# Linear attention into a routed expert layer on one core: the first batch's last products, W2's splits and two softmaxes put in other places

## The chip, the cores and the metric

The program runs on one core of a Trainium2 chip. The metric is the device time of one execution in microseconds, the median of several. The engines are named as the profile names them: PE (TensorE; PEld are its weight loads), DVE (VectorE), ACT (ScalarE), POOL (GpSimd) and SP (SyncE, which here only issues DMAs and loads registers). Each engine works through its own instructions in order, and an instruction starts when all that it waits for has been signalled.

## The reference, cut to what matters

The inputs are q, k and v of 8 batches, 8 heads, 576 positions and 64 columns, phi of 32 memory slots per head, an embedding for each of 8 experts, and the experts' weights w1 (512 by 1024) and w2 (1024 by 512).

```python
a = softmax(phi, axis=positions)
k_m, v_m = a.T @ k, a.T @ v                      # per head: 32 x 64
attn = softmax(q @ k_m.T / 8, axis=slots)        # per head: 576 x 32
x = (attn @ v_m), heads side by side             # 4608 tokens x 512
logits = (x / norm(x)) @ (emb / norm(emb)).T / tau
e, gate = argmax(logits), its softmax probability
out = gate * (relu(x @ w1[e]) @ w2[e])
```

## The kernel before, in words

A batch's 576 tokens are tiles of 128 (four, and one of 64 that overlaps: `T0`, `NT` = 5). The heads lie in two groups (`NG` = 2) of four, so the 8 x 32 slots are 2 x 128 partitions. The expert that most of a batch's tokens choose is worked out on the chip, its weights are loaded, and the whole batch goes through that one expert; tokens of other experts are counted and done at the end (`rest`), which this input does not need.

Two layers are fused with the attention's second product. `project` multiplies v_m with w1, `first` (16 steps: two halves of the tokens, eight blocks of 128 hidden columns, six matmuls each, L681) multiplies the attention weights with that and applies relu, and `second` (40 yields: the 64-token tile first, whose eight steps are the 0th to the 7th, then four tiles of eight steps) multiplies with w2. For precision each float32 operand is split into a rounded part and the rest: `wh`, `wl` of w2 (`split_w`, L651 and L652, one of eight row blocks at a time), `hh`, `hl` of the hidden layer (L684 by ACT and L687 by DVE, two per step), `gh`, `gl` of the projected w1 (L664, L665), `aT` of the attention weights (`part`, L641 by ACT or DVE and L642 by POOL).

The order of the work is written out by hand. `steps` fills two lists, and after each yield of `first` and `second` the list's entry is called, which appends instructions to the engines' queues. While batch b goes through its layers, these entries do for batch b+1 the scores' softmax (`fill`, `weigh`, `divide`, `turn`: per head group a chain on DVE, L64, L71, L73, L83 to L86, L92, with one exponential by ACT, L75), the attention's product with the values and the router's columns (`pairs`, L139, called in `visit`), the choice of the expert (`choose`, in `gather`, L208 to L212) and the load of its w1 and w2 (L442, L448), and for batch b+2 the softmax of phi (`largest` L457 on DVE, the exponential L472 on ACT, `shares` L483, and the transposes `flip`, L504, in `visit`).

What SP issues, in this order, in the first batch's second layer: `lay` writes the next batch's attention weights to DRAM (`td<-x`, L100, four DMAs per head group, behind `divide`), reads them back in token order (`ea<-td`, L104 and L106), `keep` saves two tensors (L633, L634), then the expert's number is loaded to a register (L212) and w1 (four DMAs of 512 KB, L442) and w2 follow. `project` of the next batch reads all four of w1's pieces.

The first batch has no batch before it, so it computes its own attention in pieces: tile 0 ahead of everything, tiles 1 and 2 (`attend(1, 2)`: products L119, transposes L172, `best`, then `norm`) between the halves of `project`, and tiles 3 and 4 by `attend(3, 4)` after step 2 of `first`. Its norms and gates (`late`: `root`, `gates`, six calls) follow steps 3 to 8; `idx` (L263) is on POOL. `split_w` of w2 follows step 2 (two blocks) and steps 9 to 14 (one each): POOL rounds blocks 0 to 5, ACT 6 and 7, POOL subtracts all eight.

Of the kernel before, what the change touches and what calls it, by code (L numbers as in the profile page):

```python
# [46 lines left out]
class Tokens:  # L47


    def __init__(self, k, b, pt):  # L50
        self.k, self.nc, self.b, self.pt = k, k.nc, b, pt
        wk = k.wk.tile
        self.lg = wk([P, NT, E], F32, tag="lg", name=f"lg{b}")
        self.ss = wk([P, NT], F32, tag="ss", name=f"ss{b}")
        self.s2 = wk([P, 2, NT], F32, tag="s2", name=f"s2{b}") if b else None
        self.m = wk([P, NT], F32, tag="m", name=f"m{b}")
        self.oh = wk([P, NT, E], BF16, tag="oh", name=f"oh{b}")
        self.po = {}
# [49 lines left out]
    def attend(self, *ti, pt=None, turned=True):  # L108

        k, nc, b = self.k, self.nc, self.b  # L110
        if b:
            self.open()
            self.pairs()
            return
# [12 lines left out]
    def open(self):  # L127

        self.ps = [self.pt([P, 512], f"po{self.b}_{n}") for n in range(4)]

    def pairs(self):
# [3 lines left out]
        for i in range(NT):  # L135
# [11 lines left out]
        self.room = ps[-1][:, 512 - E :]  # L147
        l2 = k.wk.tile([P, NT, E], F32, tag="l2", name=f"l2{b}")
        for n, i in enumerate((slice(0, 3), slice(3, NT))):
            for h, to in enumerate((self.lg, l2)):  # L150
                e = ps[2 * n + h][:, : 2 * d * (i.stop - i.start)].rearrange("p (i g m) -> p i m g", g=NG, m=d)
                e = e[:, :, D - D * h :][:, :, :E]
                nc.vector.tensor_reduce(out=to[:, i], in_=e, axis=AX.X, op=ALU.add)
        nc.vector.tensor_tensor(out=self.lg, in0=self.lg, in1=l2, op=ALU.add)
        self.best(*range(NT))
# [19 lines left out]
    def norm(self, *ti):  # L175
        k, nc = self.k, self.nc
        for i in ti:
            x = k.ea[:, i].rearrange("p (g k m) -> p g k m", g=NG, k=2)
            po = self.po[i] if self.b else [self.po[i].rearrange("p (g k m) -> p g k m", g=NG, k=2)[..., :D]]
            for h, y in enumerate(po):  # L180
                to = x[:, :, h] if self.b else x
# [8 lines left out]
                    accum_out=(self.s2[:, h] if self.b else self.ss)[:, i : i + 1],  # L190
# [42 lines left out]
    def root(self):  # L233
        k, nc, b, ss = self.k, self.nc, self.b, self.ss
        self.n = n = k.wk.tile([P, NT], F32, tag="n", name=f"n{b}")
        if b:
            nc.vector.tensor_tensor(out=ss, in0=self.s2[:, 0], in1=self.s2[:, 1], op=ALU.add)
# [38 lines left out]
class Kernel:  # L276
# [371 lines left out]
    def split_w(self, copy=None):  # L648
        j = self.halves
        x, h, l = self.w2s[:, j], self.wh[:, j], self.wl[:, j]  # L650
        (copy or self.nc.scalar.copy)(h, x)  # L651
        self.nc.gpsimd.tensor_tensor(out=l, in0=x, in1=h.bitcast(F32), op=ALU.subtract)  # L652
        self.halves += 1
# [89 lines left out]
    def steps(self, b, t, u):  # L743
# [4 lines left out]
        for j in range(8):  # L748
            at = first[j] if b else first[2] if j < 2 else first[7 + j]
            at.append(lambda j=j: self.split_w(self.nc.gpsimd.tensor_copy if b or j < 6 else None))  # L750
        if not b:
            late = t.late()
            first[2].append(lambda: t.attend(3, 4))
            first[3].append(lambda: t.norm(3, 4))
            first[4] += [t.total, lambda: self.load_kv(2)]

            for f in range(3, 9):
                first[f].append(lambda: next(late))
            first[12] += [lambda: self.keep(0), lambda: self.load_q(2)]
        if u:  # L760
# [19 lines left out]
            if m < B:  # L780
                for g in range(NG):
                    second[11 + 3 * g + o].append(lambda g=g: self.softmax(m, (g,)))
# [38 lines left out]
    def batch(self, b, t, u):  # L821
# [11 lines left out]
        for k, _ in enumerate(self.project(b, self.vT[b % 2]) if u else ()):  # L833
            if not b:
                for g in range(NG):
                    self.part(g, slice(HS, S) if k else slice(P, HS), self.nc.scalar.copy)
                if k:
                    t.norm(1, 2)
                else:
                    self.keys(1)  # L840
                    self.values(1)
                    t.attend(1, 2)
        if b and u:

            self.scores(b + 1)
# [255 lines left out]
```

## Time and profile before

| | us |
|---|---|
| median of 3 runs (lowest to highest) | 407.17 (406.46 to 407.32) |
| the profiled execution's own time | 406.74 |
| its span in the profile | 404.9 |
| PE busy / DVE / ACT / POOL | 393.5 / 262.3 / 157.2 / 171.2 |
| first batch's `first` begins, `second` begins | 32.38, 48.47 |
| second batch's `project` begins | 80.05 |

The span is what lies between the first and the last instruction that the profiler saw; the rest of the execution's own time lies around it. Matmuls are pipelined and their ends are modelled, so PE's busy share says little about waits of some tenths of a microsecond; the starts of its instructions in the timeline do. A timeline row gives the start, the duration, the engine, the line and the operation, and in brackets how long the engine had been idle and what ended that. PE's clock is granted at 0.998 of its upper level (2.4 GHz) over the span.

### The profile page before, as it was taken

To read this page: it belongs to the slowest core of one execution; us is meant where nothing else is said; L and a number is where in the kernel's file an instruction comes from. 1 tells how busy PE (TensorE), PEld (TensorE's weight loads), DVE (VectorE), ACT (ScalarE), POOL (GpSimd) and SP (SyncE) were. 2 spreads that over 40 slices of the span, in tenths; PEclk is the share of its full clock that TensorE was granted. 3 is DMA by queue.
4 is the path that set the end of the run, shared out by engine and by line. 5 is a ranking of instruction groups with operands and counts; after the bars stand their busy time and mean duration, and the time that the engine had idled before them with its cause. 6 is when DMAs were issued, how large, how long until landed. Compare 5 with 4: busy or idle time off the path is not lost. (4 is left out here: it accounts for less than half of the span.)

```text
span 404.9 us, 10350 instructions
## 1 busy us (share of the span) xinstructions
PE 393.5 (97%) x3933; PEld 318.5 (79%) x3933; DVE 262.3 (65%) x909; ACT 157.2 (39%) x430; POOL 171.2 (42%) x205
## 2 busy tenths in 40 slices
PE   7889999999999999999999999999999999999995
PEld 3458877798777978879787888879788897879784
DVE  4698795769664794758855795747936595745000
ACT  4366623165313633147311753137231561146110
POOL 1036563187133940369121961349303681329300
PEclk9999999999999999999999999999999999999999
DMA  8999927995679925995469926798359404790011
GB/s 265 345 363 357 375 61 183 342 358 212 149 255 386 349 46 132 346 384 234 74 215 389 387 82 160 251 388 338 56 137 361 178 2 81 249 396 6 14 53 56
DMA packets 69862, 91.24 MB, mean 225 GB/s; under 512 B 41800, under 2 KB 47688, under 8 KB 69808
## 3 DMA queue, kind: packets, MB, share of 16 engines
q1 hardware_dynamic: 66928, 82.00, 60.9%
q0 software_dynamic: 2688, 8.26, 5.8%
q8 instruction: 32, 0.52, 0.5%
q10 hardware_dynamic: 192, 0.28, 0.2%
q14 instruction: 22, 0.18, 0.1%
HBM read 71.19 MB, written 19.33 MB: 224 GB/s over the span
## 5 line engine op out<-in xcount | busy, mean ns | idle before, releaser
L681 PE MATMUL ph<-aT,gh 128*128 128x288 f32 x512 | 103.2, 297 | 0.0
L734 PE MATMUL py<-wh,hh 128*128 128x512 f32 x248 | 99.3, 400 | 0.0
L734 PE MATMUL py<-wh,hl 128*128 128x512 f32 x248 | 96.7, 390 | 0.0
L734 PE MATMUL py<-wl,hh 128*128 128x512 f32 x248 | 96.7, 390 | 0.0
L652 POOL TENSOR_TENSOR wl<-w2s,wh 128x512 fp32r<-128x512 f32 x64 | 85.1, 1330 | 5.0
L681 PEld LDWEIGHTS ph<-aT,gh 128*128 128x128 f32 x512 | 81.8, 188 | 1.7 <-DVE oh L162 0.8
L681 PE MATMUL ph<-aT,gl 128*128 128x288 f32 x256 | 75.4, 294 | 0.0
L687 DVE SCALAR_TENSOR_TENSOR hl<-ph,hh 128x288 fp32r<-128x288 f32 x128 | 55.8, 450 | 22.1 <-ACT hh L684 16.7
L739 ACT ACTIVATE ys<-py,gate 128x512 f32<-128x512 f32 (+1 forms) x39 | 25.1, 642 | 105.3 <-PE py L734 70.3
L684 ACT ACTIVATE hh<-ph 128x288 fp32r<-128x288 f32 x128 | 52.4, 417 | 31.9 <-PE ph L681 31.6
L868 POOL DMA_DIRECT2D out_dram<-ys x28 | 15.5, 553 | 106.1 <-ACT ys L739 69.4
L734 PEld LDWEIGHTS py<-wh,hh 128*128 128x128 f32 x248 | 46.5, 188 | 14.6 <-issue 4.9
L734 PEld LDWEIGHTS py<-wh,hl 128*128 128x128 f32 x248 | 46.6, 188 | 10.1
L734 PEld LDWEIGHTS py<-wl,hh 128*128 128x128 f32 x248 | 46.6, 188 | 9.0
L681 PEld LDWEIGHTS ph<-aT,gl 128*128 128x128 f32 x256 | 48.0, 188 | 0.0
L642 POOL TENSOR_TENSOR aT<-aw,aT 128x576 fp32r<-128x576 f32 (+3 forms) x20 | 23.7, 1204 | 48.4 <-DVE aT L641 42.8
L651 POOL CAST wh<-w2s 128x512 fp32r<-128x512 f32 x62 | 38.6, 622 | 1.0 <-DMA w2s<-w 0.9
L723 PE MATMUL py<-w2s,h 128*64 128x256 f32 x256 | 29.4, 382 | 0.0
L665 DVE TENSOR_TENSOR gl<-pg,gh 128x512 fp32r<-128x512 f32 x32 | 20.0, 684 | 8.7 <-ACT gh L664 8.7
L723 PEld LDWEIGHTS py<-w2s,h 128*64 128x64 f32 x256 | 17.7, 137 | 9.3 <-DVE hl L687 1.0
L472 ACT ACTIVATE ex<-ex,nm 128x576 f32<-128x576 f32 x16 | 12.3, 771 | 29.5 <-DVE nm L457 29.5
L664 ACT CAST gh<-pg 128x512 fp32r<-128x512 f32 x32 | 16.5, 599 | 10.5 <-PE pg L662 10.5
(180 smaller groups left out, 468.9 us busy)
## 6 DMA issues: line engine op xcount, KB each, us to landing
kx<-kv SPq DMA_DIRECT2D x32, 512.0 KB, 7.5
w2s<-w SPq DMA_DIRECT2D x32, 512.0 KB, 9.8
w1s<-w SPq DMA_DIRECT2D x28, 512.0 KB, 6.4
out_dram<-ys POOLq DMA_DIRECT2D x28, 256.0 KB, 6.1
qt<-qT SPq DMA_DIRECT2D x12, 576.0 KB, 8.8
ad<-aw SPq DMA_DIRECT2D x8, 576.0 KB, 12.5
td<-x SPq DMA_DIRECT2D x56, 72.0 KB, 2.1
ea<-td SPq DMA_DIRECT2D x7, 512.0 KB, 4.4
```

What stands on the lines that cost most here:

```text
L642: self.nc.gpsimd.tensor_tensor(out=al, in0=a, in1=ah.bitcast(F32), op=ALU.subtract)
L651: (copy or self.nc.scalar.copy)(h, x)
L652: self.nc.gpsimd.tensor_tensor(out=l, in0=x, in1=h.bitcast(F32), op=ALU.subtract)
L664: nc.scalar.copy(self.gh[:, g, f], ps[g])
L665: nc.vector.tensor_tensor(out=self.gl[:, g, f], in0=ps[g], in1=self.gh[:, g, f].bitcast(F32), op=ALU.subtract)
L681: nc.tensor.matmul(p, lhsT=w[:, g, fs], rhs=x[:, g, to], start=g == 0 and k == 0, stop=g == 1 and k == 2)
L684: nc.scalar.activation(self.hh[:, f, to], p, AF.Relu)
L687: nc.vector.scalar_tensor_tensor(out=self.hl[:, f, to], in0=p, scalar=0.0, in1=self.hh[:, f, to].bitcast(F32), op0=ALU.max, op1=ALU.subtract)
L723: nc.tensor.matmul(p[64 * j : 64 * j + 64], lhsT=self.h4[:, f], rhs=self.w2s[:, f, d * j : d * j + d], start=f == 0, stop=f == 7,)
L734: nc.tensor.matmul(p, lhsT=h[:, f, to], rhs=w[:, f], start=f == 0 and k == 0, stop=f == 7 and k == 2)
L739: nc.scalar.activation(y[:, :d], p, AF.Copy, scale=gate[:, i : i + 1])
L868: eng.dma_start(self.out[r : r + P], y)
```

## The change

For the first batch only: `attend(3, 4)` comes one step later and uses the 64 by 64 products of the later batches (`open`, `pairs`, `logits` for the last two tiles, then the transposes); its two square sums per tile go through `s2`. The transposes and norms of tiles 1 and 2 move behind step 0 of `first`, the second half of `project` behind step 1, so that two steps of `first` come ahead of it. `norm(3, 4)`, `total` and the six calls of `late` come one step later. All eight splits of w2 come behind the gates, one each behind steps 11 to 15 of `first` and 0 to 2 of `second`; POOL rounds blocks 0 to 2, ACT 3 to 7; POOL subtracts blocks 0 to 5, DVE 6 and 7. The maxima of phi for batch 2 are issued behind steps 0 and 1 of `second` and the exponentials behind steps 2 and 5 (before: all behind steps 18 and 21). For the later batches the only difference is that this softmax comes one step sooner (10 and 13 in place of 11 and 14).

```diff
     def attend(self, *ti, pt=None, turned=True):
-        if b:
-            self.open()
-            self.pairs()
+        if b or ti[0] == 3:
+            self.open(b)
+            if b:
+                self.pairs()
+            else:
+                self.pairs(1)
+                self.turned(*ti)
+                self.logits(1)
             return
...
-        for i in range(NT):
+        for i in range(3 * first, NT):
...
+    def logits(self, first=0):
...
-        nc.vector.tensor_tensor(out=self.lg, in0=self.lg, in1=l2, op=ALU.add)
-        self.best(*range(NT))
+        i = slice(3 * first, NT)
+        nc.vector.tensor_tensor(out=self.lg[:, i], in0=self.lg[:, i], in1=l2[:, i], op=ALU.add)
+        self.best(*range(3 * first, NT))
...
-        if b:
-            nc.vector.tensor_tensor(out=ss, in0=self.s2[:, 0], in1=self.s2[:, 1], op=ALU.add)
+        i = slice(0 if b else 3, NT)
+        nc.vector.tensor_tensor(out=ss[:, i], in0=self.s2[:, 0, i], in1=self.s2[:, 1, i], op=ALU.add)
...
-    def split_w(self, copy=None):
+    def split_w(self, copy=None, by=None):
...
-        self.nc.gpsimd.tensor_tensor(out=l, in0=x, in1=h.bitcast(F32), op=ALU.subtract)
+        (by or self.nc.gpsimd).tensor_tensor(out=l, in0=x, in1=h.bitcast(F32), op=ALU.subtract)
...
         for j in range(8):
-            at = first[j] if b else first[2] if j < 2 else first[7 + j]
-            at.append(lambda j=j: self.split_w(self.nc.gpsimd.tensor_copy if b or j < 6 else None))
+            at = first[j] if b else (first[11:] + second)[min(j, 7)]
+            copy = self.nc.gpsimd.tensor_copy if b or j < 3 else None
+            at.append(lambda j=j, copy=copy: self.split_w(copy, None if b or j < 6 else self.nc.vector))
         if not b:
             late = t.late()
-            first[2].append(lambda: t.attend(3, 4))
-            first[3].append(lambda: t.norm(3, 4))
-            first[4] += [t.total, lambda: self.load_kv(2)]
-
-            for f in range(3, 9):
+            first[3].append(lambda: t.attend(3, 4))
+            first[4] += [lambda: t.norm(3, 4), lambda: self.load_kv(2)]
+            first[5].append(t.total)
+
+            for f in range(4, 10):
                 first[f].append(lambda: next(late))
...
                 for g in range(NG):
-                    second[11 + 3 * g + o].append(lambda g=g: self.softmax(m, (g,)))
+                    if not b:
+                        second[g].append(lambda g=g: self.largest(m, g))
+                    second[10 + 3 * g if b else 2 + 3 * g].append(lambda g=g: self.softmax(m, (g,)))
...
-        for k, _ in enumerate(self.project(b, self.vT[b % 2]) if u else ()):
-            if not b:
-                for g in range(NG):
-                    self.part(g, slice(HS, S) if k else slice(P, HS), self.nc.scalar.copy)
-                if k:
-                    t.norm(1, 2)
-                else:
-                    self.keys(1)
-                    self.values(1)
-                    t.attend(1, 2)
-        if b and u:
-
-            self.scores(b + 1)
+        project = self.project(b, self.vT[b % 2]) if u else ()
+        if b:
+            list(project)
+            if u:
+                self.scores(b + 1)
+        else:
+            self.part(0, slice(P, HS), self.nc.scalar.copy)
+            next(project)
+            self.part(1, slice(P, HS), self.nc.scalar.copy)
+            self.keys(1)
+            self.values(1)
+            t.attend(1, 2, turned=False)
+            first[0] += [lambda: t.turned(1, 2), lambda: t.norm(1, 2)]
+            first[1].insert(0, lambda: list(project))
+            for g in range(NG):
+                first[1].append(lambda g=g: self.part(g, slice(HS, S), self.nc.scalar.copy))
```

## Rows read from the trace of the kernel before

**Rows 1.** The page: busy time, share of the span, instructions by engine.
```profile
PE 393.5 (97%) x3933; PEld 318.5 (79%) x3933; DVE 262.3 (65%) x909; ACT 157.2 (39%) x430; POOL 171.2 (42%) x205
```
**Rows 2.** Timeline of PE, first batch's opening: start us, us, engine, line, operation, count.
```profile
30.77 0.66 PE L172 MATMUL tt<-ident,aw 128*128 128x128 f32 x4 [0.36 <-ACT kT L551]
...
34.86 1.09 PE L119 MATMUL po<-vv,aw 128*128 128x136 f32 x8
35.78 0.60 PE L172 MATMUL tt<-ident,aw 128*128 128x128 f32 x4
36.14 0.51 PE L681 MATMUL ph<-aT,gh 128*128 128x288 f32 x2
```
**Rows 3.** Timeline of PE where the first batch's second layer meets the visit.
```profile
63.55 0.39 PE L734 MATMUL py<-wh,hl 128*128 128x512 f32 x1
64.40 0.28 PE L504 MATMUL po<-ident,ex 64*128 64x64 f32 x2 [0.46 <-ACT ex L472]
...
65.10 1.48 PE L139 MATMUL po<-vv,aw 64*64 64x72 f32 x80
```
**Rows 4.** Waits of PE over the span: us in total, times, longest us.
```profile
PE po L504 <- ACT ex L472: 0.6, 2, 0.5
```
**Rows 5.** Timeline of PE and its weight loads: `project` of the second and third batch.
```profile
80.05 2.28 PE L662 MATMUL pg<-w1s,vT 64*32 64x512 f32 x32
80.42 0.23 PEld L662 LDWEIGHTS pg<-w1s,vT 64*32 64x32 f32 x10 [0.20 <-DMA w1s<-w]
...
128.03 1.95 PE L662 MATMUL pg<-w1s,vT 64*32 64x512 f32 x32
```
**Rows 6.** L442's DMAs issued from 70 to 73 us: issue to landing.
```profile
DMA to landing us min/median/max: 6.0/7.1/8.4
```
**Rows 7.** Timeline of SP, first batch's second layer.
```profile
58.13 5.12 SPq L100 DMA_DIRECT2D td<-x  x8
65.10 0.39 SPq L104 DMA_DIRECT2D ea<-td  x1
...
70.30 2.70 SPq L442 DMA_DIRECT2D w1s<-w  x4
```
**Rows 8.** Waits of the DMA queue SP from 57 to 71 us.
```profile
SPq L100 <- DVE x L86: 14.8, 2, 13.9
```
**Rows 9.** Timeline of DVE, first batch's second layer.
```profile
49.97 0.77 DVE L64 STREAM_TRANSPOSE x<-sT 128x576 f32<-128x576 f32 x1
...
51.56 1.56 DVE L73 TENSOR_TENSOR x<-x,mx 128x576 f32<-128x576 f32 x1
...
54.63 1.51 DVE L73 TENSOR_TENSOR x<-x,mx 128x576 f32<-128x576 f32 x1
...
60.28 0.76 DVE L86 TENSOR_TENSOR x<-x,z 128x576 f32<-128x576 f32 x1
61.15 0.78 DVE L92 STREAM_TRANSPOSE aw<-x 128x576 f32<-128x576 f32 x1
...
61.98 1.37 DVE L457 TENSOR_REDUCE nm<-ex 128x1 f32<-128x576 f32 x2
```
**Rows 10.** Timeline of POOL around the first batch's splits.
```profile
44.76 0.61 POOL L651 CAST wh<-w2s 128x512 fp32r<-128x512 f32 x1
...
51.23 4.29 POOL L652 TENSOR_TENSOR wl<-w2s,wh 128x512 fp32r<-128x512 f32 x3
```
**Rows 11.** Timeline of ACT at the end of the first batch's first layer.
```profile
48.40 0.72 ACT L651 CAST wh<-w2s 128x512 fp32r<-128x512 f32 x1
48.91 0.53 ACT L684 ACTIVATE hh<-ph 128x288 fp32r<-128x288 f32 x1
```
**Rows 12.** Durations in ns, min/median/max, of two of SP's instructions, whole span.
```profile
L106 SPq DMA_DIRECT2D ea<-td x14: 509/597/1318, 65.5 to 343.8; - x14
L212 SPq TENSOR_LOAD <-seli x8: 264/280/913, 20.7 to 346.7; - x8
```
**Rows 13.** The page: a product of half a tile with its square sum.
```profile
L182 DVE CUSTOM_DVE_ANT_1 ea<-po,ea 128x128 f32<-128x128 f32 x70 | 15.3, 285 | 0.0
```

More of the change, by code (lines that the diff above doesn't have):

```diff
@@ L54, in __init__ @@
         self.ss = wk([P, NT], F32, tag="ss", name=f"ss{b}")
-        self.s2 = wk([P, 2, NT], F32, tag="s2", name=f"s2{b}") if b else None
+        self.s2 = wk([P, 2, NT], F32, tag="s2", name=f"s2{b}")
         self.m = wk([P, NT], F32, tag="m", name=f"m{b}")
@@ L125, in attend, with open, pairs @@
         self.best(*ti)
-    def open(self):
-        self.ps = [self.pt([P, 512], f"po{self.b}_{n}") for n in range(4)]
-    def pairs(self):
+    def open(self, all=True):
+        self.ps = [self.pt([P, 512], f"po{self.b}_{n}") if all or n > 1 else None for n in range(4)]
+    def pairs(self, first=0):
         k, nc, b, d, ps = self.k, self.nc, self.b, D + E, self.ps
         at = lambda i, h: ps[2 * (i // 3) + h][:, 2 * d * (i % 3) :][:, : 2 * d].rearrange("p (g m) -> p g m", g=NG)
-        for i in range(NT):
+        for i in range(3 * first, NT):
             for g in range(NG):
@@ L147, in pairs @@
         self.room = ps[-1][:, 512 - E :]
+        if not first:
+            self.logits()
+    def logits(self, first=0):
+        k, nc, b, d, ps = self.k, self.nc, self.b, D + E, self.ps
         l2 = k.wk.tile([P, NT, E], F32, tag="l2", name=f"l2{b}")
-        for n, i in enumerate((slice(0, 3), slice(3, NT))):
+        for n in range(first, 2):
+            i = slice(3, NT) if n else slice(0, 3)
             for h, to in enumerate((self.lg, l2)):
@@ L178, in norm @@
             x = k.ea[:, i].rearrange("p (g k m) -> p g k m", g=NG, k=2)
-            po = self.po[i] if self.b else [self.po[i].rearrange("p (g k m) -> p g k m", g=NG, k=2)[..., :D]]
+            two = isinstance(self.po[i], list)
+            po = self.po[i] if two else [self.po[i].rearrange("p (g k m) -> p g k m", g=NG, k=2)[..., :D]]
             for h, y in enumerate(po):
-                to = x[:, :, h] if self.b else x
+                to = x[:, :, h] if two else x
                 nc.vector.tensor_tensor_reduce(
@@ L189, in norm @@
                     op1=ALU.add,
-                    accum_out=(self.s2[:, h] if self.b else self.ss)[:, i : i + 1],
+                    accum_out=(self.s2[:, h] if two else self.ss)[:, i : i + 1],
                 )
```

## The prediction

> **What bounds the kernel now.** The page says that PE is busy for 97% of the span [rows 1], which looks like a kernel that only less matrix work can shorten. Because ends of matmuls are modelled, I read PE's timeline by starts instead, looking for places where PE stood still. In the third to last batches there are none that this change could touch: in the whole span PE waited only twice for the softmax of phi [rows 4]. So the time to be won lies in the first batch and at its border to the second, and there are three such places.
>
> First, at 30.77 the transposes of tiles 1 and 2 start after 0.36 us of idle PE [rows 2]. Second, at 64.40 the visit starts after 0.46 us in which PE waited for the exponential of phi [rows 3]. Third, and this decides: `project` of the second batch takes 2.28 us where the same 32 matmuls take 1.95 in the third, and the weight loads in it resume at 80.42, released by the DMA of w1 [rows 5]. PE is there at 80.05 and waits 0.33 us in the middle for the last of w1's four pieces. That piece was issued near 72 and needed 8.4 us, the longest of the four [rows 6, 7].
>
> So behind the first batch PE is not the only bound. A second chain arrives at the same place a little later than PE. Followed backwards: w1 is issued from 70.30 on SP; before it stand the two kept tensors and `ea<-td` from 65.10; before that the eight `td<-x`, issued from 58.13 to 63.25 [rows 7]; and these wait for DVE's L86, the last step of `divide` [rows 8], whose second instance ends at 60.28 + 0.76 = 61.04 [rows 9]. DVE in turn works from 49.97 on: `fill`, maximum, subtraction for one head group, the same for the other, then the two divides [rows 9]. Whatever DVE is given ahead of 49.97 makes w1 later; whatever PE saves before 80.05 only makes it wait longer there.
>
> **The change, part by part.** The sum is made against the profiled execution, 406.74 us (span 404.9 and 1.84 around it). The median of the runs, 407.17, is 0.43 above it.
>
> *PE's opening.* Step 0 of `first` takes the place of the idle 0.36 us, since by then PE no longer needs the copy that the transposes waited for. The products of tiles 3 and 4 now take 0.92 us (34.86 to 35.78) [rows 2]. In 64 by 64 tiles there are 2 tiles x 2 groups x 4 matmuls x 2 passes = 32 instructions; the visit's 80 take 1.48 us [rows 3], so 32 take 0.59, and 0.33 is saved at most. The array is switched to the small tiles and back, which no row prices alone; between 0 and the whole 0.33 I take half, 0.17. The two gaps together make 0.53; I take 0.45 for PE's arrival at the second layer, because the later logits and norms leave DVE a little closer to the steps (bounds 0.2 and 0.7).
>
> The Trainium skill's page "TensorEngine Tiling (Array Packing)", in "Theoretical Speedup", allows up to a factor of two for each dimension of 64, which on columns alone (72 in place of 136) would save 0.43 us here; "Key Properties" of the same page has each change of tiling mode drain the engine, which speaks against it. Rows 3 stand nearer to the second. By the first, PE's gain would be 0.7 and the end the same, as it lies ahead of the wait for w1.
>
> *Logits and norms.* Four products of half a tile at 0.285 us [rows 13] replace two whole ones, and two short additions are new. They lie on DVE beside the steps of `first`; what covers them is that PE needs a step's result only four steps later. If that cover went, under 1 us of PE's gain would go with it, again ahead of the wait for w1.
>
> *POOL.* Its splits started at 44.76 behind the gates and ended at 55.52 [rows 10]. Now it does six subtractions and three roundings from about the same moment: 3 x (0.61 + 1.3) + 3 x 1.43 = 10.0, so it ends near 55 again. The third last block is then only just in time for PE. If PE waits there, by up to a microsecond, it waits less for w1.
>
> *ACT.* One of its two roundings (0.51 from start to start, 48.40 to 48.91 [rows 11]) no longer stands before the last relu. With PE's 0.45 that puts DVE's last `hl` about 0.65 sooner, and DVE is free at 49.97 - 0.65 = 49.3. Three roundings for blocks 4 to 6 then follow on ACT, and block 6 is ready near 50.45.
>
> *DVE, ahead of `fill`.* One maximum of phi: 1.37 / 2 = 0.69 [rows 9], to 50.0. Then DVE's subtraction of block 6, queued behind it, waits for ACT until 50.45, and everything behind it waits too. The trace has no such subtraction on DVE with both inputs in SBUF. The nearest rows are two of that kind on 576 columns: L86 takes 0.76 with POOL idle, L73 takes 1.56 and 1.51 while POOL subtracts back to back [rows 9, 10]. For 512 columns that is 0.68 or 1.36. POOL is subtracting at that moment, so I take 1.36; 0.68 stays the lower end. Second maximum 0.69, subtraction of block 7 again 0.68 to 1.36. `fill` starts at 50.45 + 2 x 1.36 + 0.69 = 53.9 (lower end 52.5) where it was 49.97: +3.9 (+2.5).
>
> *DVE, behind it.* The two L73 no longer run against POOL, which is done near 55: they should take 0.8 each in place of some 1.45, which gives back 1.3 (0.65 if the first still meets POOL, as it does in the lower case). The divides end 2.6 later, or 1.9. I take 2.4. The two maxima that stood at 61.98 are gone from there, but nothing on this chain stood behind them.
>
> The Trainium skill's page "SBUF — State Buffer", "Who interferes with whom", says that VectorE and GpSimd share one pair of ports as an exclusive lock, so that the second to issue blocks until the first is done. Rows 9 and 10 agree with a slowdown of that size. By that rule a subtraction on DVE could cost up to 0.68 + 1.43 = 2.1 us, and the sum would be 1.5 us higher.
>
> *The visit.* Its wait for the exponential (0.46) goes, as both are done by 54. What is late next is `turn` of the second group: it ended at 61.93 [rows 9] and will end near 64.3, while PE wants it at 65.10 - 0.46 - 0.45 = 64.2. So about 0.1 to 0.3 of the 0.46 comes back as a new wait.
>
> *SP.* No DMA changes its place in the queue. All of it from `td<-x` on moves with L86: +2.4. In this chain stand two instructions that take unusually long in the first batch only: a small `ea<-td` at 1.318 (0.6 otherwise) and the load of the expert's number at 0.913 (0.28 otherwise) [rows 12]. Nothing shows why; if they go with the new moment, 1.35 us is taken back. I take 0.4 for that: w1 is issued and lands 2.0 us later, the last piece at 82.4.
>
> *Later batches.* The softmax one step sooner: nothing, PE has no wait there [rows 4].
>
> *Sum.* PE reaches `project` at about 79.4 instead of 80.05 and waits until 82.4 instead of 80.42. From there all is as before, 2.0 later: 406.74 + 2.0 = 408.7 for the profiled kind of run, 407.17 + 2.0 = 409.2 for the median.
>
> **The rivals.** *Faster.* w1 lands before PE wants it. Then PE keeps 0.45, the 0.46 of the visit and the 0.33 of `project`: 1.24, a median of 405.9. The place is SP's first w1 DMA: PE wins only if it is issued before 70.3, and by over 0.2% (0.8 us, about what a measurement of this kernel can tell from no change) only if by 69.5. For it: SP's two slow instructions. Against it: DVE gets 1.4 us of maxima and at least 1.4 us of subtractions ahead of `fill`, and only 1.3 + 0.65 come back. Chance 0.12.
>
> *No change.* The lower case of DVE (+1.9, or +1.2 if both L73 are freed as well) meets SP's whole slack of 1.35: w1 comes between -0.15 and +0.6, and the median is 407.0 to 407.8. Chance 0.14.
>
> *Slower still.* Each subtraction on DVE waits out one of POOL's: +1.5 on the sum less what SP takes back, about 410.3. I count this within slower, with 0.1 of its chance. The forecast's own case has 0.64.
>
> That the change does not do what it says is not to be expected of the order, as each queue runs in the order written; only the sooner softmax of the later batches is without effect.
>
> **How the numbers follow.** The likeliest case is 409.2, from 408.0 (lower DVE case, half of SP's slack) to 410.2. The range of 8 in 10 reaches down into "no change" to 407.0 and up to 410.3; what it leaves out is the faster rival and the top of the slowest. Slower by over 0.2%: 0.74; within: 0.14; faster: 0.12.
>
> **What would show it.** In the changed profile the row at 30.77 has lost its wait, and L504 its wait for the exponential. L64 starts between 52.5 and 54 with two L457 and two subtractions of `wl` on DVE ahead of it, the latter near 1.4 us. The second L86 ends near 63.4, w1's first DMA is issued near 72.3, and the weight loads of the second `project` wait about 3 us for the DMA of w1. I am wrong if w1 is issued at 70.3 or sooner, if `project` takes its 1.95 us, or if L64 starts before 51.

## The result and the profile after

The changed kernel takes 410.06 us (median of 10 runs, 409.03 to 411.86) where the kernel before, run beside it, takes 407.25 (10 runs, 405.75 to 408.29). The ratio is 1.0082, with a 95% interval of 1.0062 to 1.0102: about 3.3 us slower. The forecast was 409.2, that is +2.0, with a range up to 410.3; 407.25 x 1.0082 is 410.6. The profiled execution of the changed kernel took 411.66 (span 409.8), 1.6 above its median, while that of the kernel before lay 0.5 below its own. So the traces differ by 4.9 us, of which 1.6 to 2.1 belong to these two executions. In both traces PE's clock stands at its upper level up to the last 1.6 us (mean 0.998 in both), so the clock has no part in what they differ by.

PE's busy share on the page is 97% as before [rows 1], with 24 more matmuls and as many more weight loads:

```profile
PE 398.3 (97%) x3957; PEld 318.9 (78%) x3957; DVE 263.1 (64%) x917; ACT 158.6 (39%) x433; POOL 167.4 (41%) x200
```

What grew is seen where `project` waits. First its line in the kernel before, over the whole span: us waited, times.

```profile
  DMA w1s<-w: 0.5, 2
```

The same line (now L676) in the changed kernel:

```profile
  DMA w1s<-w: 5.8, 6
```

The timeline of PE's weight loads in the second batch's `project` of the changed kernel (answers to [rows 5]):

```profile
80.06 0.14 PEld L676 LDWEIGHTS pg<-w1s,vT 64*32 64x32 f32 x4 [0.17 <-PE tk L561]
81.00 0.14 PEld L676 LDWEIGHTS pg<-w1s,vT 64*32 64x32 f32 x4 [0.80 <-DMA w1s<-w]
83.05 0.14 PEld L676 LDWEIGHTS pg<-w1s,vT 64*32 64x32 f32 x4 [1.92 <-DMA w1s<-w]
84.15 0.19 PEld L676 LDWEIGHTS pg<-w1s,vT 64*32 64x32 f32 x16 [0.95 <-DMA w1s<-w]
```

The four loads of w1 that `project` reads, from issue to landing (answers to [rows 6]):

```profile
DMA to landing us min/median/max: 6.5/7.7/8.8
```

PE arrives at 80.06 as before (80.05), and now waits for the second, third and fourth piece of w1; it goes on behind the last at 84.15, where it was 80.42. That is +3.73, and it is there that the second batch falls behind. The chain that leads to it, in the timelines of DVE and SP (answers to [rows 7, 9]):

```profile
50.04 0.74 DVE L471 TENSOR_REDUCE nm<-ex 128x1 f32<-128x576 f32 x1
51.19 0.93 DVE L666 TENSOR_TENSOR wl<-w2s,wh 128x512 fp32r<-128x512 f32 x1 [0.40 <-ACT wh L665]
52.05 0.74 DVE L471 TENSOR_REDUCE nm<-ex 128x1 f32<-128x576 f32 x1
52.71 1.11 DVE L666 TENSOR_TENSOR wl<-w2s,wh 128x512 fp32r<-128x512 f32 x1
53.74 0.77 DVE L64 STREAM_TRANSPOSE x<-sT 128x576 f32<-128x576 f32 x1
...
55.33 1.52 DVE L73 TENSOR_TENSOR x<-x,mx 128x576 f32<-128x576 f32 x1
...
58.36 0.76 DVE L73 TENSOR_TENSOR x<-x,mx 128x576 f32<-128x576 f32 x1
...
63.27 0.76 DVE L86 TENSOR_TENSOR x<-x,z 128x576 f32<-128x576 f32 x1
...
61.12 5.42 SPq L100 DMA_DIRECT2D td<-x  x8
69.23 0.39 SPq L104 DMA_DIRECT2D ea<-td  x1
...
73.18 2.46 SPq L456 DMA_DIRECT2D w1s<-w  x4
```

The links are: end of the divides 61.04 to 64.03 (+2.99); from there to `ea<-td`, which waits for the last `td` to land, 4.06 to 5.20 (+1.14); from `ea<-td` to w1's first piece 5.20 to 3.95 (-1.25); from w1's first piece to PE going on 10.12 to 10.97 (+0.85). Sum +3.73.

Elsewhere in the first two layers, on PE (answers to [rows 2, 3]):

```profile
30.85 0.51 PE L695 MATMUL ph<-aT,gh 128*128 128x288 f32 x2
...
36.15 0.73 PE L144 MATMUL po<-vv,aw 64*64 64x72 f32 x32
36.81 0.66 PE L185 MATMUL tt<-ident,aw 128*128 128x128 f32 x4
...
64.13 0.39 PE L748 MATMUL py<-wh,hl 128*128 128x512 f32 x1
64.45 0.28 PE L518 MATMUL po<-ident,ex 64*128 64x64 f32 x2
```

The wait for the exponential is gone from the visit, and the 32 small products take 0.66 from start to start. The opening does not show in absolute times, because in this execution the whole opening runs late, from before anything that the change touches: DVE's first L92 starts at 19.23 where it was 18.29, and its turn of the next 448 columns (L92) at 28.79 where it was 27.85. Counted from the latter, the first full tile of the second layer starts 23.58 later; it was 24.22. The new opening thus saves PE 0.64.

Behind the second batch two more places are slower. In the third batch the first layer starts 3.83 later than before, and `project` of the fourth 4.18: the 16 last matmuls of `acc` took longer by 0.34 (first row the kernel before, second the changed kernel; both timelines of PE).

```profile
161.00 0.45 PE L522 MATMUL acc<-kl,eT 64*32 64x128 f32 x16
```
```profile
164.83 0.79 PE L536 MATMUL acc<-kl,eT 64*32 64x128 f32 x16
```

And the last batch's `project` takes 2.70 where it took 1.95, waiting for w1:

```profile
357.87 1.95 PE L662 MATMUL pg<-w1s,vT 64*32 64x512 f32 x32
```
```profile
362.02 2.70 PE L676 MATMUL pg<-w1s,vT 64*32 64x512 f32 x32
...
362.81 0.57 PEld L676 LDWEIGHTS pg<-w1s,vT 64*32 64x32 f32 x18 [0.62 <-DMA w1s<-w]
```

The traces' 4.9 us are so 3.73 + 0.35 + 0.75, and 0.1 of small things.

### The profile page after: what moved, and what is told of

Its sections match the earlier page's. It is cut to its first block, busy times and chain, and to the rows that moved or that the text cites. A ratio compares the mean times of both kernels' runs of the same rounds, so it can differ in the third digit from the quotient of the medians.

```text
span 409.8 us, 10406 instructions
## 1 busy us (share of the span) xinstructions
PE 398.3 (97%) x3957; PEld 318.9 (78%) x3957; DVE 263.1 (64%) x917; ACT 158.6 (39%) x433; POOL 167.4 (41%) x200
## 5 line engine op out<-in xcount | busy, mean ns | idle before, releaser
L666 POOL TENSOR_TENSOR wl<-w2s,wh 128x512 fp32r<-128x512 f32 x62 | 81.6, 1318 | 4.8
```

Source lines behind the costliest of these rows:

```text
L666: (by or self.nc.gpsimd).tensor_tensor(out=l, in0=x, in1=h.bitcast(F32), op=ALU.subtract)
```

## The experiments

Two theories were held against each other. The first is the forecast's: DVE's work ahead of `fill` makes SP's chain late, and with it w1. The second: PE itself waits somewhere else (in its new opening, for W2's blocks, in transfers). A third came up on the way. Each ratio below is to the kernel before, run on the same chip beside it (406.9 to 407.4); 0.1% is 0.4 us.

**The opening alone.** In the changed kernel W2's splits and the softmax of phi go back to their old places:

```diff
-            at = first[j] if b else (first[11:] + second)[min(j, 7)]
-            copy = self.nc.gpsimd.tensor_copy if b or j < 3 else None
+            at = first[j] if b else first[2] if j < 2 else first[7 + j]
...
-                    if not b:
-                        second[g].append(lambda g=g: self.largest(m, g))
-                    second[10 + 3 * g if b else 2 + 3 * g].append(...)
+                    second[10 + 3 * g if b else 18 + 3 * g].append(...)
```

> Of the change only the products of tiles 3 and 4 in 64 by 64 tiles and the two sooner steps of the first layer; W2's splits and the two softmaxes of phi stand where they stood before. Theory (what is put ahead of DVE's fill makes w1 late, and PE waits for it): fill starts at 49.4 to 50.0, the last piece of w1 lands at 80.0 to 80.5, and whatever PE gains in the opening is waited away there: 406.8 to 407.5. Rival (the new opening itself costs: in the changed kernel's trace step 0 of the first layer took 0.207 us per matmul and DVE's opening was 0.9 us late): 408 or more, with PE behind the kernel before at the second layer.

Measured: 1.0039 (1.0014 to 1.0064), +1.6 us, and `fill` starts at 51.94, not at 49.4 to 50.0. That is the rival's number, but not by its mechanism. PE stood still once in the first layer, and the three timelines (PE, DVE, POOL) say why:

```profile
42.66 0.53 PE L695 MATMUL ph<-aT,gh 128*128 128x288 f32 x2 [1.53 <-DVE hl L701]
...
41.13 1.11 DVE L39 TENSOR_SCALAR nrg<-nrg 128x5 int32<-128x5 int32 x1
42.16 0.44 DVE L701 SCALAR_TENSOR_TENSOR hl<-ph,hh 128x288 fp32r<-128x288 f32 x1
...
40.95 1.27 POOL L666 TENSOR_TENSOR wl<-w2s,wh 128x512 fp32r<-128x512 f32 x1
```

A step on 5 columns that takes 0.17 elsewhere took 1.11 and ended at 42.24, with POOL's subtraction (42.22). The norms now come one step later and meet POOL's early splits. So the opening and the splits' new places belong together: the later splits are what lets the opening gain.

**The splits alone**, in the kernel before: the changed lines of `split_w` and its places, nothing else.

> Of the change only the places and engines of W2's splits (POOL rounds three blocks, ACT five, POOL subtracts six, DVE two). Theory: two subtractions of 0.9 to 1.1 us on DVE and a wait for ACT put fill at 51.8 to 52.6, the divides and w1 follow by 1.3 to 2.0 us, 408.5 to 409.4. Rival (POOL's six blocks come too late and PE waits in the second layer): PE is late before 64 us by 0.3 us or more, w1 is no later than that, 407.5 to 408.2.

Measured: 1.0054 (1.0032 to 1.0076), +2.2 us, as the theory had it in number, but not by its sum. `fill` starts at 53.36, about 1 later than expected, since the two subtractions, back to back, take 2.91. PE waits about 1 us for w1, and it waits more at the visit:

```profile
66.23 0.37 PE L504 MATMUL po<-ident,ex 64*128 64x64 f32 x2 [2.57 <-ACT ex L472]
...
67.39 2.41 PE L139 MATMUL po<-vv,aw 64*64 64x72 f32 x80
```

The maxima of phi stood behind the divides, and were now late. That is what moving them ahead of `fill` cures. The 80 products behind the wait took 2.41 where they took 1.48 [rows 3], because PE's clock was granted at its lower level (1.2 GHz, 0.50 of full speed) from 66.0 to 69.4, after PE had stood still for 2.57. This row gives the stretch from 66 to 69.4, the busy time of PE, PEld, DVE, ACT and POOL, then the granted clock (0.50), the DMAs' share and GB/s:

```profile
66.00:69.40 3.40, 3.17 (x86) 3.05 (x90) 0.99 (x7) 2.04 (x7) 0.54 (x1) 0.50 0.36 39
```

From the transposes `te` to the first product behind the visit that costs 1.33 (3.34 in place of 2.01). Of the twelve executions, the three with a mean clock of 0.999 or 1.000 took 407.7 to 408.0 us, the nine with 0.992 to 0.996 took 408.9 to 410.8. So a good part of the 2.2 is the clock, which the theory did not have, and the agreement in number is in part luck.

**The maxima alone**, in the kernel before:

```diff
-                    second[11 + 3 * g + o].append(lambda g=g: self.softmax(m, (g,)))
+                    if not b:
+                        second[g].append(lambda g=g: self.largest(m, g))
+                    second[11 + 3 * g + o if b else 2 + 3 * g].append(...)
```

> Of the change only the two maxima of phi behind steps 0 and 1 of the second layer, with the exponentials behind steps 2 and 5. Theory: two maxima of 0.69 us put fill at 51.2 to 51.5, w1 lands 0.9 to 1.5 us later, the visit's wait of 0.46 us goes but PE waits that much longer for w1: 408.0 to 408.8. Rival (the chain behind fill has slack that takes it in): 406.8 to 407.4.

Measured: 0.9977 (0.9957 to 0.9996), 0.9 us faster: both ranges were missed. The trace is of the longest of its 12 executions (408.20, 1.8 above their median). In it `fill` starts at 52.17, later than expected, but the second L73 no longer met POOL (0.76 in place of 1.51), and w1's first piece was issued at 70.50, only 0.20 later than before [rows 7]:

```profile
66.73 0.39 SPq L104 DMA_DIRECT2D ea<-td  x1
67.17 1.16 SPq L106 DMA_DIRECT2D ea<-td  x2
...
70.50 2.89 SPq L442 DMA_DIRECT2D w1s<-w  x4
```

SP's two slow instructions [rows 12] were not there: from `ea<-td` to w1 3.77 in place of 5.20. Up to w1's first issue the chain thus had the slack that the prediction's rival "no change" counted on, and the visit's wait is gone. But in this execution PE still waited for w1, whose second issue took 1.20 and whose last piece landed at 81.98 (80.37 before):

```profile
82.02 0.18 PEld L662 LDWEIGHTS pg<-w1s,vT 64*32 64x32 f32 x16 [1.48 <-DMA w1s<-w]
```

So the trace shows the slack, not the gain; where the 0.9 of the median comes from is not shown.

**w1 first on SP**, in the changed kernel: the reads of td behind w1, the kept tensors behind w2.

```diff
-        if g < NG - 1:
-            return
+        if g == NG - 1 and b != 1:
+            self.back()
+
+    def back(self):
...
         self.again()
+        if u.b == 1:
+            u.back()
         self.load_w2(e)
...
-            second[22 + o] += [self.parts, lambda: self.keep(c)]
+            second[22 + o].append(self.parts)
+            second[22 + o if b else 26].append(lambda: self.keep(c))
```

> The whole change, and on SP the first batch's three small reads of the tokens' values and the two kept tensors come behind the four loads of w1 instead of ahead of them; the reads then stand ahead of w2, the kept tensors behind it. Nothing else moves, so DVE's fill is still at 53 to 54. Theory (all of the loss is w1 behind SP's queue): w1's first piece is issued near 69 as soon as the expert's number is known, the last lands before 80.2, PE does not wait for it, and the visit's 0.46 us and the 0.33 us before w1 are gained: 405.8 to 406.7. Rival (the loss is in PE's second layer or in slower transfers): 408.5 or more.

Measured: 1.0172 (1.0142 to 1.0202), +7.0 us. w1 was issued at 68.54 and had landed before PE came, as expected; but the reads of td, queued behind it, now landed late, and DVE's norms with them:

```profile
79.06 0.29 DVE L200 CUSTOM_DVE_ANT_1 ea<-po,ea 128x128 f32<-128x128 f32 x1 [7.83 <-DMA ea<-td]
```

ACT waited 11.0 for the logits behind these norms, and PE stood still for 3.06 in the middle of `project` until ACT went on. Then PE's clock was at its lower level from 86.4 to 89.8, and from the 25th product of `project` to the first layer it took 3.56 (1.99 before). The order `ea` ahead of w1 is therefore needed; what may move is the kept tensors.

**The kept tensors behind the weights**, in the changed kernel (the last three lines of the diff above).

> The whole change, and on SP the two kept tensors (ad, vd) of the first batch come behind the loads of w1 and w2; the three reads of td stay ahead of w1, since behind it (the run before) the reads landed only at 79 and DVE's norms waited 7.8 us for them. Theory (w1 is late because of what SP has ahead of it): the two kept tensors take 1.31 us of SP in the changed kernel, so w1's first piece is issued about 1.3 us sooner against the divides, the last lands 1.0 to 1.5 sooner, and the time is 408.6 to 409.2. Rival (the landing of w1 is set by the transfers themselves, or DVE's norms set the end): 409.7 to 410.5, no different from the changed kernel.

Measured: 1.0025 (1.0003 to 1.0046), 408.27. It gives back 2.3 of the 3.3 us by the ratios, more than was expected. From `ea<-td` to w1 it is now 2.50 (3.95 in the changed kernel), and the wait of L676 for w1 over the span falls from 5.8 to 4.3. SP's timeline:

```profile
68.91 0.39 SPq L104 DMA_DIRECT2D ea<-td  x1
69.35 1.19 SPq L106 DMA_DIRECT2D ea<-td  x2
71.41 2.10 SPq L456 DMA_DIRECT2D w1s<-w  x4
```

This bears out one half of the first theory: nothing but SP's order was touched, and the time followed w1. It does not show that DVE's new work is what made w1 late, as the kept tensors stood ahead of w1 before the change too.

**The same with the maxima alone**, in the kernel before.

> The kernel before with two edits alone: the two maxima of phi behind steps 0 and 1 of the second layer (exponentials behind 2 and 5), and the two kept tensors behind the loads of w1 and w2 on SP. Theory: PE keeps the 0.46 us of the visit, and w1, 1.3 us sooner on SP, makes PE wait 0.3 us or less in the second project: 405.0 to 405.8, against 406.4 with the maxima alone. Rival (SP's order is not what holds w1): 406.2 to 406.8.

Measured: 0.9976 (0.9954 to 0.9998), no different from the maxima alone. Here L662 waits for w1 neither in the second batch nor in the last: w1 is there first, so that a still earlier one buys nothing. These two versions are the ones that beat both kernels.

**No subtraction on DVE**, in the changed kernel:

```diff
-            at.append(lambda j=j, copy=copy: self.split_w(copy, None if b or j < 6 else self.nc.vector))
+            at.append(lambda j=j, copy=copy: self.split_w(copy))
```

> The whole change, but POOL subtracts all eight blocks (DVE none). Theory: without two subtractions and the wait for ACT, 2.5 us, DVE's fill starts 2.3 to 2.6 us sooner, both L73 meet POOL again and cost 1.5 more, so the divides and w1 come 0.9 to 1.3 sooner; POOL ends near 59 and PE waits 1 to 2 us for blocks 6 and 7 before the visit, which takes that much out of the wait for w1: 408.6 to 409.5. Rival (POOL's late blocks set the end through PE): 410 or more, with no wait for w1 left in project.

Measured: 1.0042 (1.0023 to 1.0061), 409.19, as expected: 1.6 of the 3.3 us come back by the ratios without DVE's two subtractions, which bears out the other half. `fill` starts at 50.15, both L73 meet POOL (1.72 and 1.51), and PE waits for POOL's last blocks (waits between 51 and 64.6):

```profile
PEld py L748 <- POOL wl L666: 1.8, 2, 1.2
...
PE py L748 <- POOL wl L666: 0.8, 1, 0.8
```

**The maxima put back**, in the changed kernel: opening and splits together.

> The whole change, but the maxima and exponentials of phi stand where they stood before (behind steps 18 and 21 of the second layer): the new opening and W2's splits together. Theory: DVE has its two subtractions but not the maxima ahead of fill, which starts 0.3 to 0.7 us sooner than in the changed kernel (the subtractions wait for ACT anyway); the visit waits 2.5 to 3.5 us for the exponentials, as with the splits alone: 409.3 to 410.3. Rival (the maxima, not the subtractions, delay the divides): 408 or less.

Measured: 1.0109 (1.0080 to 1.0138), +4.4 us, 2 more than the middle of what was expected. The visit's wait is the 2.82 that was foreseen; the splits' two subtractions, back to back, take 1.36 in the mean (0.96 and 1.76), the upper price of the prediction.

```profile
69.18 0.28 PE L518 MATMUL po<-ident,ex 64*128 64x64 f32 x2 [2.82 <-ACT ex L486]
```

Here too PE's clock was at its lower level for a while: from 30.0 to 33.4, after PE had stood still for 2.38 until the first batch's w1 came. From the first `tk` product to the fourth of `first` it took 3.41, where the opening alone took 1.83. That 1.6 is most of the 2 in this execution; the mean clock of all six lies between 0.991 and 0.995 (0.996 to 0.999 in the changed kernel), and where the others lost it is not recorded.

**The second tile's output held back**, in the changed kernel, because it lies among the `td` writes:

```diff
+            elif not b and i == 1:
+                self.held = lambda: eng.dma_start(self.out[r : r + P], y)
...
+        if b == 1:
+            first[3].append(self.held)
```

> The whole change, and the 256 KB of output of the first batch's second tile are sent in the second batch's first layer instead of at once. In the changed kernel that transfer (issued 64.86, landed 67.3 to 68.3) lies between the last td writes (landed 66.4 to 69.1), which in the kernel before were done (64.97) when the same transfer was issued (65.21). Theory (the last part of w1's delay is td sharing the DMA engines with that output): the last td lands 1.0 to 1.6 us sooner against the divides, the reads and w1 follow by as much, 408.7 to 409.3. Rival (td's own small pieces are slow): 409.7 to 410.5.

Measured: 1.0088 (1.0065 to 1.0111), 410.20: no gain. The `td` writes did land faster, 2.3 at the median as in the kernel before (2.2) in place of 3.2 (first fence the changed kernel, second this one; issue to landing):

```profile
DMA to landing us min/median/max: 2.6/3.2/3.6
```
```profile
DMA to landing us min/median/max: 2.3/2.3/3.8
```

and the read `ea<-td`, which waits for them, came 0.5 sooner behind the divides (4.70 in place of 5.20). But SP's two small reads now took 1.89 in place of 1.33, the load of the expert's number 0.92, and w1 was issued at 73.45. What the sharing between the output and `td` costs is therefore small, and it was taken back behind it.

**Both edits together**, held output and kept tensors.

> The whole change with both edits: the second tile's output sent in the second batch and the two kept tensors behind w1 and w2 on SP. Theory: both edits shorten the same chain, so they add: w1 lands about 2.3 us sooner against the divides, PE waits 0.5 to 1.2 us for it, 406.9 to 407.7. Rival (what is left is not on that chain): 408 or more.

Measured: 1.0023 (1.0001 to 1.0045): the kept tensors' gain and no more. The rival's range.

**A version put together** from the parts:

```diff
-            at = first[j] if b else (first[11:] + second)[min(j, 7)]
+            at = first[j] if b else (first[11:] + second)[min(j, 8) - 1] if j else first[2]
...
-            at.append(lambda j=j, copy=copy: self.split_w(copy, None if b or j < 6 else self.nc.vector))
+            at.append(lambda j=j, copy=copy: self.split_w(copy))
```

with the two edits of the run before.

> A version put together from what the runs showed: the change's opening, maxima and roundings, both edits of the run before, and no subtraction on DVE; one of W2's blocks is split behind step 2 of the first layer as before the change and the other seven behind the gates, so that POOL ends near 56. Theory: DVE's fill starts within 0.5 us of the kernel before (two maxima against the sooner opening), w1 lands before PE wants it or within 0.5 us of that, and PE keeps the opening's 0.6 and the visit's 0.46: 405.2 to 406.2. Rival (POOL's early split delays DVE in the opening as with the opening alone, or its last blocks delay PE): 406.5 to 407.5.

Measured: 1.0015 (0.9995 to 1.0034), not told from the kernel before: the rival's range. PE waits neither at the visit nor for w1 in the second and the last batch; but one early split was enough to hold up DVE in the opening (`oh`, L175, takes 1.12 in place of 0.17), and the opening's gain was gone.

**The number of PE's instructions.** By now one thing stood out. From the first product of the last batch's `project` to the first layer, the four profiled kernels with the old opening took 3.37 each; the nine with the new one took 3.37 once and 3.44 to 4.68 otherwise, whatever else they did. The later batches' code differs by nothing that PE waits for; but PE has 49 more instructions. This row of the DMA view, for 351 to 355.5 us of the changed kernel, has no counterpart between 347 and 350.5 us of the kernel before, where w1 for the last batch is issued:

```profile
q8 instruction: 1, 0.02, 1.8%
```

One transfer of 16 KB in the instruction queue, at 351.9. The second of w1's four issues, next on SP, took 1376 ns; in the kernel before none took over 365 (durations min/median/max in ns, the kernel before first).

```profile
L442 SPq DMA_DIRECT2D w1s<-w x4: 332/342/365, 347.4 to 349.1; - x4
```
```profile
L456 SPq DMA_DIRECT2D w1s<-w x4: 332/348/1376, 351.6 to 354.2; - x4
```

The Trainium skill, in "Runtime: NRT & Kernel Launch", section "Instruction fetch mechanics", has code come in blocks of 16 KiB, 256 instructions, over a queue of the sequencer's own, at a cost that is "mostly hidden". The size agrees with the row. Whether the cost is hidden was tried in both directions: in the kernel before, the first warm-up matmuls are cut to add 48 PE instructions; in the changed kernel all of them are, to come to 259 more than before, so that blocks of that size begin almost where they did (there `parts` is `n`).

```diff
-        for _ in range(n):
-            self.nc.tensor.matmul(hot, lhsT=self.ones, rhs=x, start=True, stop=True)
+        parts = 8 if n == 11 else 0
+        for i in range(n):
+            for j in range(4 if i < parts else 1):
+                to, y = (hot[:, j * w : j * w + w], x[:, 0]) if i < parts else (hot, x)
+                self.nc.tensor.matmul(to, lhsT=self.ones, rhs=y, start=True, stop=True)
```

> The kernel before with its work unchanged, but 8 of its first 11 warm-up matmuls (512 columns, ahead of all data) cut into four of 128 columns: 24 more matmuls and 24 more weight loads on PE, as many as the change's 64 by 64 tiles add (24 and 25). Seen in the runs so far: every kernel with the new opening has 49 more PE instructions, and in the trace a 16 KB transfer of the instruction queue then comes just ahead of the second load of w1 for the last batch (SP's instruction takes 0.85 to 1.38 us in place of 0.35), whose project takes 3.88 to 4.68 us in place of 3.37; and batch 2's products acc take 2.60 in place of 2.26. Theory (what moves these is where PE's code is reloaded, so the number of PE instructions alone brings them): the last project 3.9 or more and 0.7 to 1.3 us lost, 407.8 to 408.6. Rival (they come from the change's work): 3.37 stays, 406.7 to 407.5.

Measured: 1.0025 (1.0006 to 1.0043), 408.10: 1.0 us (0.2 to 1.8 by the interval) for 48 instructions that do nothing for the result. The last `project` on PE in this kernel:

```profile
358.67 2.77 PE L665 MATMUL pg<-w1s,vT 64*32 64x512 f32 x32
```

and the issues of its w1:

```profile
L445 SPq DMA_DIRECT2D w1s<-w x4: 332/349/1012, 348.2 to 350.5; - x4
```

The third batch's `acc` (from its first product to the next work), expected at 2.60, stayed at 2.26; the second batch's took 3.11 in place of 2.77 instead, and the second `project` waited 0.6 longer for w1, whose second issue took 1032 ns with a code transfer 0.3 ahead of it. With 1.0 us for the instructions the opening alone can be accounted for, as an estimate: 1.0, and 1.53 for the wait, less its gain of 0.64, is 1.9 against the 1.6 measured.

> The whole change, with all 35 warm-up matmuls of the opening cut into four of 128 columns: 210 more PE instructions on the change's 49, 259 together, so that 16 KB blocks of 256 instructions of 64 bytes begin 3 instructions off from where they do in the kernel before. The warm-up works on no data of the result. Theory (PE's code reloads): the last project takes 3.37 again, batch 2's acc 2.26, and 0.7 to 1.2 us come back, 408.8 to 409.5, while the wait for w1 in the second batch stays. Rival (the change's work): 409.8 to 410.5.

Measured: 1.0099 (1.0071 to 1.0128). In the later batches it went as expected: the third batch's `acc` is at its old length, and the last `project` is as in the kernel before (PE's timeline; none of the four issues of its w1 took over 364 ns).

```profile
361.80 1.95 PE L679 MATMUL pg<-w1s,vT 64*32 64x512 f32 x32
```

But the time did not fall, and its range was missed. A code transfer now comes at 64.8, among the `td` writes of the first batch. The longest of their issues takes 1662 ns:

```profile
L100 SPq DMA_DIRECT2D td<-x x7: 302/498/1662, 60.7 to 64.9; - x7
```

and PE's weight loads go on behind w1 at 84.19, although this execution's `fill` started at 52.97:

```profile
84.19 0.18 PEld L679 LDWEIGHTS pg<-w1s,vT 64*32 64x32 f32 x16 [1.09 <-DMA w1s<-w]
```

What was saved behind was lost in front.

## Why the prediction was right in sign and short in size

*What bounds the kernel.* Right: PE's gain ahead of 80.05 was waited away at w1, and moving only SP's kept tensors brought 2.3 us back.

*PE's opening.* 0.64 against 0.45, inside its bounds; the 32 small products save 0.26 of the 0.92 in place of 0.17. That logits and norms are covered holds only while POOL is quiet: with the old splits the cover broke and cost 1.53. The prediction gave under 1 us for that.

*POOL.* It ended at 56.2, and the second layer up to the visit took 11.76 in place of 11.48, a wait of 0.3 where up to 1 was foreseen.

*DVE ahead of `fill`.* Foreseen 53.9, found 53.74; in the six profiles with this same order it lies between 52.65 and 53.74. That it came out so close is luck: 0.94 of it is this execution's late opening, and 52.8 without it is near the lower end. The subtractions took 0.93 and 1.11, between the two prices; 1.36 is their mean where they follow each other. The rival "slower still", in which each waits out one of POOL's (up to 2.1), did not come about, although the time came out near its number. That number is itself a slip: 1.5 on a sum of 409.2, in which SP's 0.4 is already taken off, makes 410.7.

*DVE behind it.* The give-back was half of what was taken: the first L73 still met POOL (1.52), only the second was freed (0.76). The divides end 2.99 later, 2.05 if the opening's lateness of 0.94 is taken off; foreseen 2.4.

*The visit.* Its wait went, and no new one came: the foreseen 0.1 to 0.3 is not there.

*SP.* Foreseen -0.4; found +0.74 between the divides and PE. This is one of the two steps that failed. The prediction says of SP's two slow instructions that nothing shows why. For the slow `ea<-td` the trace of the kernel before does show something: a transfer of 16 KB in the instruction queue begins at 65.47, and the read that takes 1.318 is issued at 65.54. In the changed kernel such a transfer begins at 61.25, and the `td` issued at 61.49 takes 1.367. The rows of the DMA view (65.2 to 66.9 us of the kernel before, 61.1 to 62.9 of the changed kernel):

```profile
q8 instruction: 1, 0.02, 3.2%
```
```profile
q8 instruction: 1, 0.02, 3.5%
```

So that slow instruction did not go, it moved to the `td` writes. (With the output held back such a transfer, at 68.72, met the read again, at 68.76: 1.26.) What was saved behind `ea<-td` (-1.25; half of it is the load of the expert's number, beside which no such transfer stands) was lost again in `td` landing later (+1.14) and in w1 taking 0.85 longer from issue to PE going on. The last is not explained; over the runs in which PE waits for w1 that figure lies between 9.3 and 11.5. The piece of w1 that PE waited for in the kernel before is of the same kind: its issue, at 72.00, took 1.00 where the other three took 0.33 to 0.38, with a transfer begun at 71.75.

*The sum.* The other step that failed is "From there all is as before, 2.0 later". It is not: the third batch's `acc` and the last `project` add 0.35 and 0.75. In the traces the wait for w1 is thus worth 2.79, with the late opening's 0.94 taken off, where 2.0 was foreseen, and what lies behind it 1.1 where nothing was; one execution, 1.6 above its median, does not tell how the median's 3.3 divides between them. What both steps leave out is that 49 more PE instructions move the code transfers onto other work. By the kernel before with 48 more of them that costs 1.0 us by itself. If this simply adds, the ratio of the changed kernel to that one is 1.0082 / 1.0025 = 1.0057, 2.3 us, near the forecast's chain of +2.0. That it adds is not shown: the changed kernel with its blocks moved back was no faster, and no number of instructions was tried at which the transfers miss both the `td` writes and w1. Counting the instructions of each *queue* was done for DMAs; for PE's code it was not. The later batches' softmax did cost nothing, as foreseen: first layer to next `project` takes 43.96 to 44.00 in the fourth to sixth batch of both kernels.

What stays open: why the maxima alone are 0.9 us faster rather than slower; how much of the splits' loss, alone and with the opening, is PE's clock over all executions; and the 0.34 of the third batch's `acc`. Seven of the nine profiles with the new opening and uncut warm-ups show some of it, the kernel before with 48 more instructions does not. In the six that show all of it a code transfer begins 0.05 to 0.22 us ahead of `acc`, but so it does with the splits alone and the maxima alone, which show none.

## What to carry to other kernels

Where two chains arrive at the same place a little apart, a gain on the one that comes first is worth nothing, and work put ahead on the other is paid as far as that chain has no slack: look for which queue issues what the bound engine waits for last, and shorten that. Parts of a change may be cures for one another (later splits for the opening, earlier maxima for the later splits), so price them together, and try the one that stands alone: here the maxima without the rest are 0.2% faster than before (0.0 to 0.4%). Look at the granted clock of each run before its loss is put down to an edit: three of these traces have a stretch of 3.4 us at the lower level, which no expectation had in it. In a kernel tuned to tenths of a microsecond, adding instructions to an engine is itself a change elsewhere; compare against a kernel with the same number of them before a loss is put down to the work.

## What the runs showed of the hardware that was not expected

A DMA issue on SP is often slow where a transfer of PE's code begins just ahead of it. w1's second issue for the last batch, 0.35 otherwise, took 0.84 to 1.38 where a 16 KB transfer of the instruction queue began 0.3 to 0.4 us ahead, in eight of the kernels profiled. Counted over all fifteen traces from 40 us on, without the reads of phi: of the 65 issues that start within 0.4 us behind such a transfer's begin 49 took over 0.8 us, of the other 2927 only 79. That these transfers are PE's code is read from their number: 32 in the span of each other kernel, 33 in the one with 259 more PE instructions. The reads of phi are left out because from 100 us on 165 of 180 of them take 0.99 or more, with or without a transfer. Shifting PE's instructions and nothing else brought the slow issue in one run and took it away in another; by what path, the trace does not say. The Trainium skill, in "Runtime: NRT & Kernel Launch", section "Instruction fetch mechanics", has the cost of crossing such a block "mostly hidden"; in this kernel 48 instructions more cost 1.0 us.

A DVE step of 0.17 takes until POOL's subtraction ends (41.13 to 42.24, POOL until 42.22), even on 5 columns. The Trainium skill, "SBUF — State Buffer", section "Who interferes with whom", has the two share an exclusive lock, and these rows agree with it; so a tiny step can cost as much as a large one.

Three reads (512 KB, and twice 64 KB) that were issued from 70.92 to 72.46, behind four pieces of 512 KB, let DVE go on only at 79.06; the same reads ahead of them took under 5 us at the median.

PE's clock fell to its lower level for 3.4 us in three traces: with the splits alone, after PE had stood still for 2.57; with w1 first, after 3.06; with the maxima put back, after 2.38. The same work then took 1.3 to 1.6 us longer. In the last of these PE stood still for 2.82 later on, and the clock did not fall.
